# Moving one pair of maxima, one transpose and four scores in the instruction order of an attention kernel

## The chip, the cores and the metric

The kernel runs on one core of a Trainium2 chip. The metric is the device time of one execution in microseconds (us): the median of three executions, 1805.07 us, between 1804.39 and 1807.82.

## What is computed

Four layers in turn on a sequence of 2048 rows of width 640, with 32 heads of 20 columns each. Layers A are linear attention. Layers B split the sequence into four segments of 512 rows; each segment has causal softmax attention within itself, and reads a memory that the earlier segments filled. The part of the reference that the change touches is the attention inside a segment:

```
for s in range(N):
    qs, ks, vs = q[:, :, s], k[:, :, s], v[:, :, s]
    logits = jnp.einsum("bhqd,bhkd->bhqk", qs, ks) * scale + mask
    p = _softmax(logits, axis=-1)
    a_dot = jnp.einsum("bhqk,bhkd->bhqd", p, vs)
    ...
    o = g * a_mem + (1.0 - g) * a_dot
```

## The kernel before

**Two streams on one core.** `attend` runs the softmax attention; `dense` runs everything else (projections, memories, the A layers, output products). `run` interleaves the two. After each stretch of attention, which yields the constant SLOT = 2420, it lets the dense stream go on until its own counted cost has caught up. So PE's order is written by hand: the `manual_schedule` of `build` fixes PE's order to that of the code, while a scheduler orders the instructions of the other engines and of SP's queue.

**Groups.** In each of the two B layers, each of the four segments has eight groups of four heads, so 64 groups in all. A group goes through these operations:

- `stacks` (L985) loads the queries and keys, `qs` and `ks`, with four DMAs in SP's queue. There are three buffers of each.
- `row_max` ("max", L999 on PE, L1006 on DVE) computes plain scores into PSUM banks on PE; DVE reads them and keeps each row's maximum in `mg`. Entries 0 and 2 have two matmuls of 512 columns, entries 1 and 3 have two of 384 and two of 128, entry 4 has four of 256. Each entry takes two banks.
- `split_max` ("split", L1015 and L1016 on DVE) writes the maxima in two f16 parts into a small tile.
- `max_rows` ("rows", L1024 on PE, L1026 on ACT, L1029 in SP's queue) turns these parts with a transpose on PE (`pm`, one bank); ACT copies them to `mt`, and two small DMAs put them into spare rows of `qs`. From then on a score matmul subtracts the maximum itself.
- `scores` ("exp", L1041 on PE, L1045 on ACT, L1052 on POOL) computes transposed scores into a bank, ACT takes the exponential into a tile `pe`, POOL masks the diagonal. Entries 0 and 1 have two banks each, with one matmul of 512 columns in each bank; entries 2 and 3 have two banks each, with matmuls of 384 and 128 columns; entry 4 has two banks, each with two matmuls of 256.
- `weigh` ("sum", L1068) multiplies the values by the exponentials, four heads side by side, into one bank `pv`: part 0 has 512 columns, part 1 384, part 3 128, part 2 256. Only part 2 reads the tiles of "exp" 4.
- `evacuate` ("copy", L1074 on ACT) and `normalize` ("out", L1081 on PE, L1084 and L1091 or L1088 on DVE) bring the result back.

**The order.** An iteration of `attention` works on three groups at once, the newest (0), the one before (1) and the one before that (2), in three stretches, given by a table:

```python
STRETCHES = [[("exp", 4, 2), ("max", 0, 0), ("max", 1, 0), ("rows", 0, 1), ("sum", 0, 2), ("sum", 1, 2), ("sum", 3, 2),
              ("sum", 2, 2), ("copy", 0, 2)],
             [("out", 0, 2), ("max", 2, 0), ("max", 3, 0), ("exp", 0, 1), ("exp", 1, 1)],
             [("exp", 2, 1), ("exp", 3, 1), ("max", 4, 0), ("split", 0, 0), ("load", 0, 0)]]
```

The first number is the entry, the second the group. The maxima that a group's third stretch splits are turned by "rows" in the first stretch of the next iteration; "exp" 0 in its second stretch is the first that needs them.

**Banks.** PSUM has eight banks for all of this and for the dense stream as well:

```python
    def bank(self):
        return self.ps.tile([P, 512], F32, tag="ps", name="ps", bufs=8)
```

A matmul that opens a bank waits until ACT or DVE has read what lay there last. Dense work on PE around these places are the projections (L374, L388), transposes (L313, L876) and memory products (L443, L557, L884).

Of the kernel before, what the change touches and what calls it, by code (L numbers as in the profile page):

```python
# [51 lines left out]
EXPS += [[((0, a, 2, 0), (1, a, 2, 256)) for a in range(2)]]  # L52


STRETCHES = [[("exp", 4, 2), ("max", 0, 0), ("max", 1, 0), ("rows", 0, 1), ("sum", 0, 2), ("sum", 1, 2), ("sum", 3, 2),
              ("sum", 2, 2), ("copy", 0, 2)],
             [("out", 0, 2), ("max", 2, 0), ("max", 3, 0), ("exp", 0, 1), ("exp", 1, 1)],
             [("exp", 2, 1), ("exp", 3, 1), ("max", 4, 0), ("split", 0, 0), ("load", 0, 0)]]


# [70 lines left out]
class Kernel:  # L131
# [965 lines left out]
    def attention(self, segs):  # L1097
# [3 lines left out]
        while n < NSEG * NG or prev or old:  # L1101
# [7 lines left out]
            n += 1  # L1109
            for stretch in STRETCHES:  # L1110
                for op, k, back in stretch:
# [216 lines left out]
```

## Time and profile before

| | |
|---|---|
| median of three executions | 1805.07 us |
| the profiled execution, its own time | 1807.6 us |
| its span, from the first to the last instruction | 1805.9 us |
| PE busy in it | 1699.7 us, 94% |
| DVE, ACT, POOL busy | 66%, 54%, 29% |
| mean granted clock of TensorE | 0.993 |
| attention's matmuls | from 348.9 us to 1779.0 us |

"PE" is matmuls, "PEld" weight loads, "DVE" VectorE, "ACT" ScalarE, "POOL" GpSimd, and "SPq" the DMA queue of SyncE. A row of the waits reads: who waited, at which tile and line, for whom; then the sum of those waits in us, how often, and the longest. A row of the groups reads: line, engine, operation, tiles written <- read, shape, count; then us busy and mean ns of one; then the idle time of the engine just before them, and what ended it. A row of the timeline reads: start in us, length in us, engine, line and operation, and in brackets the idle time before it.

### The profile page before, as it was taken

What the parts mean: (1) busy time and instruction counts of PE and PEld (TensorE: products, weight loads), DVE (VectorE), ACT (ScalarE), POOL (GpSimd) and SP (SyncE); (2) the same over time, 40 slices, a digit from 0 to 9 for tenths busy, and PEclk for the clock granted to TensorE, in tenths of its full rate; (3) what the DMA queues carried; (4) which work ended last, traced back from release to release, by engine and by line L of the source; (5) the groups of instructions that cost most, each with busy time, mean ns of one, the idle gap of its engine ahead of it and who ended that gap; (6) DMA issues with size and microseconds to landing.
All of it is one profiled execution on the core that took longest, in us unless ns stands there. A gap on an engine that the chain in (4) does not pass through costs nothing.

```text
span 1805.9 us, 36393 instructions
## 1 busy us (share of the span) xinstructions
PE 1699.7 (94%) x13032; PEld 1053.8 (58%) x13032; DVE 1185.8 (66%) x3856; ACT 967.7 (54%) x1818; POOL 521.2 (29%) x982
## 2 busy tenths in 40 slices
PE   6999999999999999999989999999989999999998
PEld 4666666654565566455546777666446545644555
DVE  8554444577777677658764466737777777777773
ACT  4454433356546645567656553333665565565664
POOL 1533450012123312333342211221421432233442
PEclk9999999999999999999999999999999999999999
DMA  7332353412322322342211303433122222223432
GB/s 251 142 135 97 139 182 112 141 64 76 108 68 66 108 93 74 114 160 95 79 41 38 110 30 118 174 112 124 56 93 78 97 87 95 96 78 101 132 105 88
DMA packets 118333, 187.61 MB, mean 104 GB/s; under 512 B 13948, under 2 KB 79612, under 8 KB 115848
## 3 DMA queue, kind: packets, MB, share of 16 engines
q1 hardware_dynamic: 105896, 142.68, 24.5%
q0 software_dynamic: 3040, 21.63, 3.3%
q10 hardware_dynamic: 9216, 20.98, 3.0%
q8 instruction: 103, 1.69, 0.4%
q14 instruction: 78, 0.64, 0.1%
HBM read 106.05 MB, written 78.64 MB: 102 GB/s over the span
## 4 chain that ended last, share of the span: by engine, by line
PE 74%; DVE 12%; ACT 6%; issue 3%; POOL 2%; DMA 2%; SPq 0%; ACTq 0%; DVEq 0%; POOLq 0%
PE ps L388 32%; PE ps L374 15%; PE ps L1068 7%; DVE junk L1006 5%; PE ps L313 3%; PE ps L1041 3%; PE ps L557 3%; ACT pe L1045 3%; PE ps L443 2%; PE ps L999 2%; PE ps L884 1%; PE ps L1081 1%; PE ps L723 1%; POOL e L414 1%; DVE nat L849 1%
## 5 line engine op out<-in xcount | busy, mean ns | idle before, releaser
L1006 DVE CUSTOM_DVE_ANT_0 junk<-ps,maskw 128x512 bf16<-128x512 f32 (+3 forms) x1024 | 498.7, 487 | 83.1 <-PE ps L999 26.5
L1045 ACT ACTIVATE pe<-ps,lsc 128x512 f32<-128x512 f32 x640 | 394.1, 693 | 114.6 <-PE ps L1041 112.1
L1052 POOL TENSOR_SCALAR_AFFINE_SELECT pe<-pe 128x256 f32<-128x256 f32 (+1 forms) x640 | 233.7, 371 | 433.6 <-ACT pe L1045 428.0
L388 PEld LDWEIGHTS <-xT 128*128 128x128 f16 x2880 | 282.1, 99 | 121.0 <-issue 9.2
L388 PEld LDWEIGHTS <-oT 128*128 128x128 f16 x1920 | 185.8, 98 | 82.8 <-issue 7.9
L1068 PE MATMUL ps<-pe,v 128*32 128x512 f32 (+3 forms) x2048 | 158.1, 439 | 13.1 <-ACT pe L1045 6.8
L1041 PE MATMUL ps<-qs,ks 62*128 62x384 f16 (+3 forms) x1024 | 133.2, 300 | 24.3 <-DVE mg L1006 11.9
L388 PE MATMUL ps<-w_Bo,oT 128*128 128x320 f16 x960 | 142.3, 301 | 3.2 <-ACT oT L317 1.2
L374 PE MATMUL ps<-xT,w_Bq 128*128 128x512 f16 x600 | 141.5, 382 | 0.7 <-DVE oT L318 0.4
L388 PE MATMUL ps<-w_Bv,xT 128*128 128x320 f16 x960 | 140.9, 301 | 0.1
L388 PE MATMUL ps<-w_Ak,xT 128*128 128x320 f16 x960 | 138.4, 302 | 0.5 <-ACT r L402 0.5
L374 PE MATMUL ps<-xT,w_Bk 128*128 128x512 f16 x600 | 138.8, 379 | 0.0
L999 PE MATMUL ps<-ks,qs 60*128 60x512 f16 (+3 forms) x1024 | 112.5, 297 | 8.6 <-ACT pe L1045 4.1
L1068 PEld LDWEIGHTS ps<-pe,v 128*32 128x32 f32 x2048 | 66.0, 110 | 82.6 <-issue 62.6
L849 DVE SCALAR_TENSOR_TENSOR nat<-ps,nat 128x512 f16<-128x512 f32 x80 | 55.2, 690 | 86.2 <-ACT nat L848 82.2
L414 POOL TENSOR_SCALAR e<-e 128x320 f32<-128x320 f32 (+1 forms) x52 | 82.1, 1579 | 88.7 <-ACT e L410 84.7
L848 ACT ACTIVATE nat<-ps 128x512 f16<-128x512 f32 x80 | 48.0, 600 | 93.3 <-PE ps L374 73.0
L374 PEld LDWEIGHTS <-w_Bq 128*128 128x128 f16 x600 | 56.8, 98 | 69.7 <-issue 9.7
L374 PEld LDWEIGHTS <-w_Bk 128*128 128x128 f16 x600 | 57.0, 98 | 66.4 <-issue 5.9
L1074 ACT ACTIVATE oTf<-ps,cg 128x512 f32<-128x512 f32 x64 | 43.9, 687 | 92.1 <-PE ps L1068 92.0
L421 ACT ACTIVATE v<-ps 128x320 f32<-128x320 f32 x96 | 41.8, 437 | 94.9 <-PE ps L388 91.2
L336 POOL TENSOR_TENSOR rs<-rs,mhalf 128x1 f32<-128x1 f32 x48 | 26.4, 552 | 226.3 <-DVE rs L335 213.5
(220 smaller groups left out, 2677.8 us busy)
## 6 DMA issues: line engine op xcount, KB each, us to landing
x<-xn ACTq DMA_DIRECT2D x48, 320.0 KB
qs<-qd SPq DMA_DIRECT2D x128, 120.0 KB
ks<-kd SPq DMA_DIRECT2D x128, 120.0 KB
xo<-x SPq DMA_DIRECT2D x48, 320.0 KB
pqi<-pqd SPq DMA_DIRECT2D x32, 320.0 KB
qd<-nat SPq DMA_DIRECT2D x40, 256.0 KB
kd<-nat SPq DMA_DIRECT2D x40, 256.0 KB
x<-in_A_x SPq DMA_DIRECT2D x16, 320.0 KB
```

The lines of the kernel that those rows point to most:

```text
L313: nc.tensor.transpose(pt[:, (c - c0) * P:(c - c0 + 1) * P], src[:, c * P:(c + 1) * P], self.ident)
L374: nc.tensor.matmul(p, w[:, c, a, t * P:(t + 1) * P], xT[:, c, b, :], start=k == 0, stop=k == 3 * C - 1)
L388: nc.tensor.matmul(p, xT[:, c, a, i * P:(i + 1) * P], w[:, c, b, n * HN:(n + 1) * HN], start=k == 0, stop=k == 3 * C - 1)
L414: nc.gpsimd.tensor_scalar(e, e, 1.0, eps, op0=OP.min, op1=OP.add)
L557: nc.tensor.matmul(p, xs[:, i, a, c * P:(c + 1) * P], pk[i][:, b, cols], start=k == 0, stop=k == 3 * NT - 1)
L849: nc.vector.scalar_tensor_tensor(nat[:, 1], p, QK_SHIFT, nat[:, 0], op0=OP.mult, op1=OP.subtract)
L999: nc.tensor.matmul(bs[par][:, a:a + n], qs[r, p, i * P:(i + 1) * P], ks[r, p, :n], start=True, stop=True)
L1006: nc.vector.tensor_tensor_reduce(junk[:, :n], bs[par][:, a:a + n], self.maskw[:, SEG - n:], 1.0, NEG, OP.add, OP.max, G["mg"][:, par, p, i ...
L1041: nc.tensor.matmul(b[:, a:a + n], ks[r, p, j * P:(j + 1) * P], qs[r, p, j * P:], start=True, stop=True)
L1045: nc.scalar.activation(e, b, AF.Exp, scale=self.lsc)
L1052: nc.gpsimd.affine_select(d, d, pattern=pat, compare_op=OP.is_ge, fill=0.0, base=0, channel_multiplier=-1)
L1068: nc.tensor.matmul(G["pv"][32 * h4:32 * h4 + 32, j * P:], v[j][:, h * E1:h * E1 + 32], G.pop((p, par, j)), start=j == 0, stop=j == 2, skip ...
```

## The change

Three entries of the table change their places; no operation is added or dropped. In the first stretch, "rows" goes behind "sum" 0, and "max" 2 comes in from the second stretch, as the last entry. In the second stretch the scores "exp" 0 and 1 stand ahead of "max" 3.

```diff
-STRETCHES = [[("exp", 4, 2), ("max", 0, 0), ("max", 1, 0), ("rows", 0, 1), ("sum", 0, 2), ("sum", 1, 2), ("sum", 3, 2),
-              ("sum", 2, 2), ("copy", 0, 2)],
-             [("out", 0, 2), ("max", 2, 0), ("max", 3, 0), ("exp", 0, 1), ("exp", 1, 1)],
+STRETCHES = [[("exp", 4, 2), ("max", 0, 0), ("max", 1, 0), ("sum", 0, 2), ("rows", 0, 1), ("sum", 1, 2), ("sum", 3, 2),
+              ("sum", 2, 2), ("copy", 0, 2), ("max", 2, 0)],
+             [("out", 0, 2), ("exp", 0, 1), ("exp", 1, 1), ("max", 3, 0)],
              [("exp", 2, 1), ("exp", 3, 1), ("max", 4, 0), ("split", 0, 0), ("load", 0, 0)]]
```

On PE, at the end of a first stretch (`m` is the tile with the split maxima, `v` a tile of values, + is new and - is old):

```order
 L999 MATMUL ps<-ks_2760,qs 128x128
+L1068 MATMUL ps<-pe,v_79 32x512 x4
 L1024 LDWEIGHTS m_4094
 L1024 MATMUL pm<-ident_70,m_4094 32x128
-L1068 MATMUL ps<-pe,v_79 32x512 x4
 L1068 MATMUL ps<-pe,v_80 32x384 x4
 L1068 MATMUL ps<-pe,v_82 32x128 x4
 L1068 MATMUL ps<-pe,v_81 32x256 x4
+L999 LDWEIGHTS qs
+L999 MATMUL ps<-ks_2760,qs 128x512
```

The transpose L1024 has moved behind the four matmuls of the first weighing, and the two plain scores of 512 columns (the second one follows in the same form) stand behind the last weighing.

On PE, in the second stretch that follows:

```order
 L1081 MATMUL ps<-ident,oTf 128x128 x4
-L999 LDWEIGHTS qs
-L999 MATMUL ps<-ks_2760,qs 128x512
...
+L1041 LDWEIGHTS ks_2759
+L1041 MATMUL ps<-qs,ks_2759 128x512
...
 L999 LDWEIGHTS qs
 L999 MATMUL ps<-ks_2760,qs 128x384
```

The four scores L1041 follow the transposes of `normalize` directly; the plain scores of 384 and 128 columns, which stood ahead of them, now end the stretch.

In SP's queue, where the scheduler sets the order, around the two DMAs of the turned maxima (L1029):

```order
 L985 DMA ks_2760<-kd 60x2x512
-L985 DMA qs<-qd 60x2x512
-L1029 DMA qs<-mt 2x8x128 x2
-L985 DMA qs<-qd 60x2x512
-L985 DMA ks_2760<-kd 60x2x512
+L985 DMA qs<-qd 60x2x512 x2
+L985 DMA ks_2760<-kd 60x2x512
+L1029 DMA qs<-mt 2x8x128 x2
```

All four loads of a later group now stand ahead of the two small DMAs, where two of the four stood ahead before. Counted over the whole queue, that is so in 42 of the 64 groups now and in 7 before.

## The prediction

> **What bounds the kernel now.** I read the page first: PE is busy nearly all the time, so only the time in which it stands idle can be won, since no work is added or taken away.
>
> ```profile
> span 1805.9 us, 36393 instructions
> PE 1699.7 (94%) x13032; PEld 1053.8 (58%) x13032; DVE 1185.8 (66%) x3856; ACT 967.7 (54%) x1818; POOL 521.2 (29%) x982
> ```
>
> That leaves 1805.9 - 1699.7 = 106.2 us. Next the waits of PE alone, for whom it waits there:
>
> ```profile
> PE ps L1041 <- DVE mg L1006: 11.9, 26, 0.8
> PE ps L313 <- DMA x<-in_A_x: 10.9, 1, 10.9
> PE pm L1024 <- DVE m L1016: 8.3, 12, 0.9
> ...
> PE ps L1068 <- ACT pe L1045: 6.8, 18, 0.7
> PE ps L1068 <- POOL pe L1052: 4.4, 7, 1.2
> ...
> PE ps L1041 <- DMA qs<-mt: 2.0, 1, 2.0
> ```
>
> The largest wait in the attention is that of scores (L1041) for DVE's reading of maxima (L1006). A score does not use a new group's maxima: it waits for the bank. The second row is the start of the kernel, which the change does not touch. Then the groups with shapes kept apart, where the number behind the second bar is PE's idle time just before them:
>
> ```profile
> L1068 PE MATMUL ps<-pe,v 128*32 128x512 f32 x512 | 68.5, 603 | 9.0 <-ACT pe L1045 6.8 <-ACT xn L465 0.6 <-DVE mg L1006 0.5
> L1041 PE MATMUL ps<-qs,ks 62*128 62x512 f16 x256 | 66.8, 377 | 23.0 <-DVE mg L1006 11.6 <-DMA qs<-mt 2.0 <-DVE otok L1088 1.9
> L1041 PE MATMUL ps<-qs,ks 62*128 62x384 f16 x256 | 37.3, 330 | 1.0 <-ACT pe L1045 1.0
> L1024 PE MATMUL pm<-ident,m 128*32 128x128 f16 x64 | 14.5, 226 | 12.2 <-DVE m L1016 8.3 <-ACT r L412 1.2 <-ACT v L421 0.8
> ```
>
> The 512-column scores are those of the second stretch (entries 0 and 1): 23.0 us. Those of 384 columns, in the third stretch, have 1.0. So the second stretch itself makes the wait. The transpose of the maxima has 12.2 us, and the first weighing just behind it 9.0. These 44.2 us are what the change works on. One iteration shows how they arise, PE first, from the end of a first stretch (L1041 with 256 columns) to the scores of the second:
>
> ```profile
> 1590.00 0.40 PE L1041 MATMUL ps<-qs,ks 62*128 62x256 f16 x4
> 1590.23 0.60 PE L999 MATMUL ps<-ks,qs 60*128 60x512 f16 x6
> 1590.77 0.23 PE L1024 MATMUL pm<-ident,m 128*32 128x128 f16 x1
> 1591.32 2.36 PE L1068 MATMUL ps<-pe,v 128*32 128x512 f32 x32 [0.33 <-ACT pe L1045]
> 1593.62 1.47 PE L374 MATMUL ps<-xT,w_Bq 128*128 128x512 f16 x6
> 1594.92 0.60 PE L1081 MATMUL ps<-ident,oTf 128*128 128x128 f32 x4
> 1595.45 0.61 PE L999 MATMUL ps<-ks,qs 60*128 60x512 f16 x6
> 1595.90 0.38 PE L1041 MATMUL ps<-qs,ks 62*128 62x512 f16 x2
> 1597.10 0.79 PE L1041 MATMUL ps<-qs,ks 62*128 62x512 f16 x2 [0.82 <-DVE mg L1006]
> ```
>
> and DVE in the same time (its last reading of the first stretch, then what follows):
>
> ```profile
> 1590.65 0.69 DVE L1006 CUSTOM_DVE_ANT_0 junk<-ps,maskw 128x512 bf16<-128x512 f32 x1
> 1591.49 0.69 DVE L1006 CUSTOM_DVE_ANT_0 junk<-ps,maskw 128x512 bf16<-128x512 f32 x1
> ...
> 1594.20 0.08 DVE L1006 DVE_READ_ACCUMULATOR2_ANT mg<- 128x1 f32 x1
> 1595.56 0.26 DVE L1084 RECIPROCAL rc<-ps 128x16 f32<-128x16 f32 x1 [1.28 <-PE ps L1081]
> 1595.75 0.69 DVE L849 SCALAR_TENSOR_TENSOR nat<-ps,nat 128x512 f16<-128x512 f32 x1
> 1596.36 0.68 DVE L1006 CUSTOM_DVE_ANT_0 junk<-ps,maskw 128x512 bf16<-128x512 f32 x1
> 1596.96 0.08 DVE L1006 DVE_READ_ACCUMULATOR2_ANT mg<- 128x1 f32 x1
> ```
>
> The old second stretch opens 1 + 2 + 2 + 4 = 9 banks (out, maxima 2 and 3, scores), one more than there are. The third score therefore takes a bank whose maxima are read in the same stretch: DVE ends that at 1597.04, PE starts at 1597.10. Just before, DVE had stood idle for 1.28 us.
>
> **Term 1, the second stretch.** With maxima 2 gone ahead, the stretch opens 1 + 4 + 2 = 7 banks, and the scores come before the two of maxima 3. Maxima 2 fall into DVE's hole: its readings end at 1594.28, and two of 512 columns, which follow each other at 1591.49 - 1590.65 = 0.84 us, take 1.7 us, so they would end at 1596.0. The third score is due at 1595.90 + 0.38 = 1596.28, less 0.61 - 0.38 = 0.23 for the maxima 3 that no longer stand ahead: just in time, even if it took one of their banks. From 23.0 us go the 2.0 for a DMA, which the change does not cure, and the 1.0 that the 384-column scores still have: 20.0 is the most; 0 is the least, if the wait only moves (second rival). I take 17, near the upper end, less 3 for iterations where dense work fills DVE's hole. Two rows of ACT in the first stretch, the exponentials of exp 4 and the copy to `mt`:
>
> ```profile
> 1590.49 1.27 ACT L1045 ACTIVATE pe<-ps,lsc 128x512 f32<-128x512 f32 x2 [0.39 <-PE ps L1041]
> 1591.65 0.25 ACT L1026 ACTIVATE mt<-pm 32x128 f16<-32x128 f16 x1
> ```
>
> The two banks more that this stretch now takes are free by the time: ACT has read those of exp 4 at 1590.49 + 1.27 = 1591.76, the last weighing ends at 1593.68; I cost them at nothing. Maxima 3 start later by the scores' length, 0.38 + 0.79 us, and the split needs them one stretch on. That too costs nothing as long as dense work (here L374) lies between; if not, it comes back at L1024, less the 1.07 us that now cover it (below).
>
> **Term 2, rows behind the first weighing.** The 512-column weighing covers 68.5 / 64 = 1.07 us per group, more than the longest wait of 0.9 for the parts (`m`); so the 8.3 us vanish, as does the wait for the second bank: what the pair now needs first is only one bank, that of the old transpose, whose waits of 12.2 - 8.3 = 3.9 us stay. 12.2 + 9.0 - 3.9 = 17.3 is the most. But in this stretch a chain runs beside PE: exp 4, ACT, POOL, last weighing.
>
> ```profile
> PEld ps L1068 <- POOL pe L1052: 18.9, 49, 1.7
> ```
>
> In 49 iterations the weights of a weighing already wait for POOL, 0.39 us each on average. PE that comes sooner may only wait there: the least is 0. I take 10, nearer the upper end because PE itself idles for POOL only 4.4 us in 7.
>
> **Term 3, the maxima's way to the scores.** Transpose, ACT, two DMAs, then the scores. In the iteration above, SP's queue:
>
> ```profile
> 1590.42 0.32 SPq L985 DMA_DIRECT2D ks<-kd  x1
> 1590.91 0.32 SPq L985 DMA_DIRECT2D qs<-qd  x1
> 1591.92 1.28 SPq L1029 DMA_DIRECT2D qs<-mt  x2
> 1593.26 0.41 SPq L985 DMA_DIRECT2D qs<-qd  x1
> 1593.71 0.46 SPq L985 DMA_DIRECT2D ks<-kd  x1
> ```
>
> The transpose comes 1.07 us later. But ACT was busy with the exponentials until 1591.76 anyway, so `mt` starts not at 1591.65 but at about 1590.77 + 1.07 + 0.23 = 1592.07: 0.4 later. ACT waits 0.3 us for it; queued behind is the copy of `pv` (L1074), which needs the last weighing's end anyway. The scores come 0.2 sooner. So of 1595.90 - 1591.92 = 3.98 us from issue to scores, 3.4 stay. What the DMAs need is bounded by the shortest distance that I found without a wait, issue 954.05 to scores 957.53, 3.48 us:
>
> ```profile
> 954.05 1.27 SPq L1029 DMA_DIRECT2D qs<-mt  x2
> ```
> ```profile
> 957.53 0.60 PE L1041 MATMUL ps<-qs,ks 62*128 62x512 f16 x4
> ```
>
> So the margin is between 0.1 below zero and some tenths above. Also, two more loads of SP's queue now stand ahead: 0.41 + 0.46 us of issue, which fit in the time that SP waits for `mt` (from 1591.23 to 1591.92, and 0.4 more). What they carry goes ahead of the rows. At their size, and the best rate on the page,
>
> ```profile
> GB/s 251 142 135 97 139 182 112 141 64 76 108 68 66 108 93 74 114 160 95 79 41 38 110 30 118 174 112 124 56 93 78 97 87 95 96 78 101 132 105 88
> ...
> qs<-qd SPq DMA_DIRECT2D x128, 120.0 KB
> ```
>
> that is up to 2 x 120 / 251 = 1.0 us, at least 0 where they were away before. The Trainium skill, "DMA: Bandwidth & Descriptors", section "Queues, rings and completion order", speaks against this change: on each DMA engine descriptors are consumed in ring order. By that rule the rows would wait out the loads, and the whole 1.0 us would count in every group: 1805 - 27 + 70 = 1848. No row here shows such a delay by itself. I take 3 us in all (a few groups short by some tenths); ends 0 and 64 x (3.48 - 3.4 + 1.0) = 70 us.
>
> **The sum.** 17 + 10 - 3 = 24 us. I hand a quarter back: dense steps behind each removed stall wait for ACT and DVE with margins that the stall had widened. 18 us remain. The profiled execution's span falls from 1805.9 to 1788 (its own time 1807.6 to 1790); on the median, 1805.07 - 18 = 1787.
>
> **Rivals.** *The rows arrive too late (slower).* If the scores wait 0.5 us more in every group, half of the 1.0 above, that is 32 us against 18 won: 1805 + 14 = 1819. For it: the window shrinks in every group, and the loads moved ahead. Against it: one wait of 2.0 us in 64 groups today, and ACT takes up half the delay. It decides where issue to landing takes over about 3.3 us.
>
> *DVE's work only moves (little faster).* No reading gets shorter; if DVE reaches maxima 2 late, or maxima 3 hold up the split, half of term 1 and most of term 2 come back: 1805 - 7 = 1798. For it: DVE 66% busy over the span, with dense work put between maxima by the scheduler. Against it: the hole of 1.28 us. The Trainium skill, "TensorEngine Tiling (Array Packing)", section "PSUM Bottleneck", says that packing speeds up TensorE but not the reading of PSUM; by that rule this case would win.
>
> *Nothing is left.* The scheduler orders ACT, DVE and SP anew throughout, and new small waits eat what was won: 1805.
>
> **How the numbers follow.** Forecast (1776 to 1795) 0.58; DVE's work moves (1795 to 1801) 0.17; nothing left 0.12; rows too late 0.13. About 0.2%, 3.6 us, is what a measurement can tell from no change here. So faster 0.75, same 0.12, slower 0.13. For 8 in 10 I leave out what lies under 1774 (nearly all of both upper ends, 37 us, won) and most of the late rows: 1774 to 1806.
>
> **What would show it.** Right: idle before the 512-column scores falls from 23.0 to about 5, before L1024 and the 512-column weighing from 21.2 to about 10, with PE's busy time unchanged near 1700. Wrong: a row of scores waiting for the DMA of `mt` over 10 us (first rival); scores still waiting for DVE, or L1024 for the split (second); the weighing waiting for POOL well over 4.4 us (term 2).

## The result, and the profile after

The changed kernel takes 1765.53 us (median of six executions, 1763.05 to 1769.35), the kernel before 1806.03 us beside it. The ratio is 0.9768, with a 95% interval of 0.9754 to 0.9782: 40 us faster, where 18 were forecast and 1774 was the range's lower end. The direction was right, the size was not. One of the six executions of the kernel before took 2189.03 us; without it their median is 1805.12 us. The profiled execution of the changed kernel took 1769.35 us.

The head of the page after, the span first, then busy time, share and instructions of each engine:

```profile
span 1767.6 us, 36360 instructions
PE 1683.3 (95%) x13032; PEld 1050.2 (59%) x13032; DVE 1195.1 (68%) x3856; ACT 971.2 (55%) x1818; POOL 517.4 (29%) x982
```

The span fell by 1805.9 - 1767.6 = 38.3 us. PE's idle time fell from 106.2 to 1767.6 - 1683.3 = 84.3, which is 21.9 of them. The other 16.4 us came out of PE's *busy* time, with the same 13032 matmuls. The prediction had said that nothing could be won there. PE's largest waits after:

```profile
PE ps L313 <- ACT xh L361: 19.7, 5, 11.3
PE pm L1024 <- DVE m L1016: 5.0, 2, 3.2
PE ps L1041 <- DMA qs<-mt: 3.7, 2, 2.9
PE ps L999 <- DVE mg L1006: 3.6, 10, 0.5
PE ps L1068 <- POOL pe L1052: 3.4, 7, 1.4
...
PE ps L999 <- ACT pe L1045: 3.1, 10, 0.6
```

The wait of scores for DVE's reading of maxima, 11.9 us before, has left the list. The first row lies ahead of the attention, in the kernel's first 121 us; before, the same line waited 10.9 us for a DMA and 7.7 for ACT. The groups by shape (the number behind the first bar is busy time, the one behind the second the idle time just before):

```profile
L1068 PE MATMUL ps<-pe,v 128*32 128x512 f32 x512 | 68.2, 603 | 4.6 <-ACT r L412 1.7 <-ACT pe L1045 0.9 <-ACT r L402 0.7
L999 PE MATMUL ps<-ks,qs 60*128 60x384 f16 x256 | 51.6, 324 | 6.1 <-DVE mg L1006 2.3 <-ACT pe L1045 1.6 <-DVE tmp L1091 0.8
L1041 PE MATMUL ps<-qs,ks 62*128 62x512 f16 x256 | 40.4, 385 | 3.8 <-DMA qs<-mt 3.7
L999 PE MATMUL ps<-ks,qs 60*128 60x128 f16 x256 | 33.5, 216 | 0.0
L1024 PE MATMUL pm<-ident,m 128*32 128x128 f16 x64 | 14.1, 221 | 5.2 <-DVE m L1016 5.0 <-DVE oT L318 0.2
```

The 512-column scores lost 23.0 - 3.8 = 19.2 us of idle time, and 66.8 - 40.4 = 26.4 us of busy time, while one of them still takes 385 ns (377 before). So they are not shorter; they overlap more. One iteration after, on PE, shows how:

```profile
1545.14 0.60 PE L999 MATMUL ps<-ks,qs 60*128 60x512 f16 x6
1545.67 1.06 PE L1068 MATMUL ps<-pe,v 128*32 128x512 f32 x8
1546.55 0.22 PE L1024 MATMUL pm<-ident,m 128*32 128x128 f16 x1
1546.56 1.51 PE L1068 MATMUL ps<-pe,v 128*32 128x384 f32 x24
1548.00 0.39 PE L999 MATMUL ps<-ks,qs 60*128 60x512 f16 x2
1548.32 2.21 PE L388 MATMUL ps<-w_Bv,xT 128*128 128x320 f16 x15
1550.37 0.60 PE L1081 MATMUL ps<-ident,oTf 128*128 128x128 f32 x4
1550.90 0.61 PE L1041 MATMUL ps<-qs,ks 62*128 62x512 f16 x4
1551.34 0.38 PE L999 MATMUL ps<-ks,qs 60*128 60x384 f16 x4
```

All four scores stand in one row of 0.61 us, and the next matmul starts 1551.34 - 1550.90 = 0.44 us after the first. Before, they stood in two rows of 0.38 and 0.79 us with 0.82 between. A score uses 62 rows of PE, and the scores of a pair use different halves (rows from 0 and from 64), so two run at a time. Counted over the records of all 64 groups, the fourth score started 0.99 us after the first before, and 0.25 after: 0.74 x 64 = 47 us, of which the trace books less than half as idle.

The rest is a wait too. Each score opens a bank of its own, so the fourth waits for another bank than the third. In the iteration of the prediction the third started at 1597.10, and the fourth 0.79 - 0.38 = 0.41 us later, at 1597.51. In between, at 1596.96 + 0.49 = 1597.45, DVE ended its reading of the bank of `normalize`:

```profile
1596.96 0.49 DVE L1091 TENSOR_TENSOR tmp<-ps,rc 128x320 f32<-128x320 f32 x1
```

By the records of the kernel before, the fourth score lagged the third in 60 of the 64 groups, and in 59 of these it started 0.04 to 0.05 us after an instruction of DVE or ACT that it waits for had ended; in nearly half of the groups the third had not waited at all. In all, the fourth lagged the third by 28.3 us before and by 1.2 after. Of the 28.3 us only 6.5 were idle time; for the other 21.8 the third score ran, and PE counted as busy. In the same way the third started 18.7 us later behind the second than it does now, of which 13.5 were idle and 5.2 lay under the first pair. So 21.8 - 1.2 + 5.2 = 25.8 of the 26.4 us of busy time that went were waits under a score that still ran.

The transpose L1024 shows the same on a smaller scale: it now lies inside the weighings' rows; before, it ran out alone and PE then stood.

### The profile page after: what moved, and what is told of

Read it like the earlier page. It is cut to its first block, busy times and chain, and to the rows that moved or that the text cites. A ratio compares the mean times of both kernels' runs of the same rounds, so it can differ in the third digit from the quotient of the medians.

```text
span 1767.6 us, 36360 instructions
## 1 busy us (share of the span) xinstructions
PE 1683.3 (95%) x13032; PEld 1050.2 (59%) x13032; DVE 1195.1 (68%) x3856; ACT 971.2 (55%) x1818; POOL 517.4 (29%) x982
## 3 DMA queue, kind: packets, MB, share of 16 engines
q1 hardware_dynamic: 105896, 142.68, 25.5%
## 4 chain that ended last, share of the span: by engine, by line
PE 73%; DVE 12%; ACT 6%; issue 3%; DMA 3%; POOL 2%; SPq 0%; ACTq 0%; DVEq 0%; POOLq 0%
PE ps L388 31%; PE ps L374 15%; PE ps L1068 6%; DVE junk L1006 4%; PE ps L1041 3%; PE ps L313 3%; PE ps L999 3%; ACT pe L1045 3%; PE ps L557 3%; PE ps L443 3%; PE ps L884 1%; PE ps L1081 1%; PE ps L723 1%; DMA qs<-mt 1%; DVE st L331 1%
## 5 line engine op out<-in xcount | busy, mean ns | idle before, releaser
L1052 POOL TENSOR_SCALAR_AFFINE_SELECT pe<-pe 128x256 f32<-128x256 f32 (+1 forms) x640 | 229.6, 365 | 453.6 <-ACT pe L1045 449.3
L999 PE MATMUL ps<-ks,qs 60*128 60x384 f16 (+3 forms) x1024 | 128.8, 298 | 12.5 <-DVE mg L1006 3.6
L1041 PE MATMUL ps<-qs,ks 62*128 62x512 f16 (+3 forms) x1024 | 107.4, 301 | 5.4 <-DMA qs<-mt 3.7
L999 PEld LDWEIGHTS <-qs 60*128 60x128 f16 x1024 | 51.1, 94 | 82.5 <-issue 55.1
```

The costliest lines, as they stand in the source:

```text
L999: nc.tensor.matmul(bs[par][:, a:a + n], qs[r, p, i * P:(i + 1) * P], ks[r, p, :n], start=True, stop=True)
L1041: nc.tensor.matmul(b[:, a:a + n], ks[r, p, j * P:(j + 1) * P], qs[r, p, j * P:], start=True, stop=True)
L1052: nc.gpsimd.affine_select(d, d, pattern=pat, compare_op=OP.is_ge, fill=0.0, base=0, channel_multiplier=-1)
```

## The experiments

**Theory A**: a matmul that has to wait also loses its overlap with its neighbours, and that loss is counted as busy; the missing half of the gain is the pairs of scores. **Rival B**: only idle time counts, and what the forecast missed came from somewhere else, from the rows' new place above all. Times are set against the kernel before on the same chip (1806.61, 1806.47 and 1806.71 us in the three sets). The profiles of all experiments but the one with scores between transposes have line numbers one lower (L1040 is L1041 here, L998 is L999, L1023 is L1024).

### The rows alone

```diff
-... ("max", 1, 0), ("rows", 0, 1), ("sum", 0, 2), ("sum", 1, 2), ...
+... ("max", 1, 0), ("sum", 0, 2), ("rows", 0, 1), ("sum", 1, 2), ...
```

> Only the transpose of the maxima moves behind the first weighing; the second stretch stays as it was. Theory A (a score that waits for a bank also falls out of its pair, and what it loses then is counted as PE busy): only term 2 comes, 7 to 11 us faster than before, near 1797; the 512-column scores keep about 67 us busy and about 23 us idle. Rival B (only PE's idle time counts, and what the forecast missed came from elsewhere, the rows' move with its new order on ACT and SP's queue above all): about 25 us faster, near 1781.

Measured: 1788.33 us, ratio 0.9895 (0.9878 to 0.9911), 18.3 us faster. Neither theory had it: A said 7 to 11, B 25. The page's head and two groups:

```profile
span 1790.2 us, 36392 instructions
PE 1693.4 (95%) x13032; PEld 1048.7 (59%) x13032; DVE 1185.6 (66%) x3856; ACT 971.6 (54%) x1818; POOL 519.8 (29%) x982
```
```profile
L1040 PE MATMUL ps<-qs,ks 62*128 62x512 f16 x256 | 66.8, 377 | 24.5 <-DVE mg L1005 11.3 <-DMA qs<-mt 3.5 <-DVE otok L1087 1.9
L1023 PE MATMUL pm<-ident,m 128*32 128x128 f16 x64 | 14.0, 219 | 0.3 <-DVE oT L317 0.3
```

The scores stayed as they were, 66.8 us busy, as A had it. Idle time fell by 106.2 - (1790.2 - 1693.4) = 9.4 us, near term 2 as forecast; the other 6.3 us of the 15.7 by which the span fell in the profiled execution (the longest of the four) are busy time once more. Counted over the records, the transposes ran with nothing beside them for 7.7 us in the kernel before (0.12 us in each group, between the maxima that had run out and the weighing that waited) and for 0.3 us here. Read so, A holds in a wider form than it was put: not only in pairs, but at any matmul that still runs when a wait begins. That is read from the records alone; no run parts these 6.3 us from the rest of what moved.

### Maxima 2 alone

```diff
-             [("out", 0, 2), ("max", 2, 0), ("max", 3, 0), ("exp", 0, 1), ("exp", 1, 1)],
+             [("out", 0, 2), ("max", 3, 0), ("exp", 0, 1), ("exp", 1, 1)],
```

with `("max", 2, 0)` put at the end of the first stretch.

> Only maxima 2 move to the end of the first stretch; maxima 3 still stand ahead of the scores, and the rows stay in the old place. The second stretch then opens 7 banks before it has to wait for one of its own. Theory A: about 25 us faster than before, near 1781; busy time of the 512-column scores falls from 66.8 to 40 to 45 us and their idle time to about 6. Rival B: the idle time falls in the same way, busy time hardly, and the gain is 12 us or less, near 1794.

Measured: 1780.40 us, ratio 0.9855 (0.9839 to 0.9872), 26.2 us faster. The groups:

```profile
L1040 PE MATMUL ps<-qs,ks 62*128 62x512 f16 x256 | 42.7, 376 | 3.7 <-DMA qs<-mt 1.8 <-DVE mg L1005 0.9 <-DVE tmp L1090 0.4
L1023 PE MATMUL pm<-ident,m 128*32 128x128 f16 x64 | 14.6, 228 | 16.9 <-DVE m L1015 13.2 <-ACT r L411 1.4 <-ACT pkt L877 0.6
```

Idle time of the scores fell by 19.3 us and busy time by 24.1, as A said. B allowed 12 us in all; it falls here. The transposes' idle time rose from 12.2 to 16.9 us, that for the split from 8.3 to 13.2.

### The scores ahead of the maxima, alone

```diff
-             [("out", 0, 2), ("max", 2, 0), ("max", 3, 0), ("exp", 0, 1), ("exp", 1, 1)],
+             [("out", 0, 2), ("exp", 0, 1), ("exp", 1, 1), ("max", 2, 0), ("max", 3, 0)],
```

> Only the order within the second stretch changes: scores, then maxima 2, then maxima 3. The bank that is short is then short for the maxima (L999). Theory A: the pairs of the scores are whole, their busy time falls to about 40 us; the last maxima wait instead, part of it as idle time at L999 and part as broken pairs of the matmuls of 384 and 128 columns, so 15 to 25 us faster, near 1785. Rival B: the wait only moves, idle time at L999 rises by 10 us or more, and the gain is under 8 us, near 1800.

Measured: 1807.30 us, ratio 0.9999 (0.9989 to 1.0008): no change. B's number came true, and idle time moved to L999 as it said; but busy time, which B leaves where it was, moved with it:

```profile
L998 PE MATMUL ps<-ks,qs 60*128 60x384 f16 x256 | 62.2, 324 | 14.4 <-ACT pe L1044 9.5 <-DVE mg L1005 1.7 <-DVE oT L317 0.6
L998 PE MATMUL ps<-ks,qs 60*128 60x128 f16 x256 | 39.5, 218 | 0.0
L1040 PE MATMUL ps<-qs,ks 62*128 62x512 f16 x256 | 39.4, 383 | 2.4 <-DMA qs<-mt 2.4
```

In the kernel before, maxima 3 had these rows:

```profile
L999 PE MATMUL ps<-ks,qs 60*128 60x384 f16 x256 | 45.6, 321 | 2.0 <-ACT pe L1045 0.9 <-DVE oT L318 0.6
...
L999 PE MATMUL ps<-ks,qs 60*128 60x128 f16 x256 | 30.1, 216 | 0.0
```

The scores won 27.4 us of busy and 20.6 of idle time. Maxima 3, now last, lost 62.2 - 45.6 + 39.5 - 30.1 = 26.0 of busy and 14.4 - 2.0 = 12.4 of idle time, and maxima 4 and the transposes a few more. Here too the busy part is in the main a wait under a running matmul: by the records the second matmul of 384 columns lags the first by 18.3 us in all, by 0.2 in the kernel before, and in 54 of 64 groups it starts as an instruction of ACT or DVE that it waits for has just ended. The whole loss, with its busy part, went to the next pair that lacked a bank. A's forecast of the time was wrong: I had taken broken pairs of maxima to be cheaper.

### The change without the rows

The changed table, with `("rows", 0, 1)` back in front of `("sum", 0, 2)`.

> The whole change but for the rows, which stay behind maxima 1. Theory A: all of term 1 with the pairs, about 30 us faster than before, near 1775, some 8 to 11 us above the changed kernel; 512-column scores near 40 us busy, 4 idle, and L1024 with the 512-column weighing near 21 us idle as before. Rival B: 15 us faster or less, near 1790.

Measured: 1777.00 us, ratio 0.9832 (0.9817 to 0.9847), 29.6 us faster, as A said. The scores stand at 39.6 us busy and 2.0 idle. The transposes and the weighing behind them wait 17.8 + 8.2 = 26.0 us, more than the 21.2 of before, which A had expected:

```profile
L1067 PE MATMUL ps<-pe,v 128*32 128x512 f32 x512 | 70.8, 622 | 8.2 <-ACT pe L1044 5.5 <-DVE mg L1005 0.9 <-ACT xn L464 0.6
L1023 PE MATMUL pm<-ident,m 128*32 128x128 f16 x64 | 14.6, 228 | 17.8 <-DVE m L1015 15.0 <-ACT r L411 1.4 <-ACT r L401 0.5
```

The prediction feared that maxima 3, later by the scores' length, would hold up the split. Little of the rise is theirs: with maxima 2 alone moved, and maxima 3 in their old place, the same two rows already stand at 16.9 + 8.6 = 25.5 us. What makes the rest of it was not tried by itself. The rows' new place covers most of these waits in the full change (5.2 + 4.6).

### Seven banks

```diff
-        return self.ps.tile([P, 512], F32, tag="ps", name="ps", bufs=8)
+        return self.ps.tile([P, 512], F32, tag="ps", name="ps", bufs=7)
...
-        pt = self.ps.tile([P, 1024], F16, tag="ps", name="pm", bufs=8)
+        pt = self.ps.tile([P, 1024], F16, tag="ps", name="pm", bufs=7)
```

> The changed kernel with seven PSUM banks instead of eight, so that the second stretch is one bank short again, as it was before the change. Theory A: the lost time shows in two ways, as idle time before matmuls that open a bank and as broken pairs, with PE's busy time in the rows of scores and maxima (L1041, L999) at least 15 us up; the kernel comes near the old one, 1795 or more. Rival B: busy time stays within 5 us, all of the loss is idle time.

Measured: 1810.73 us, ratio 1.0025 (1.0015 to 1.0035): one bank is worth more than the whole change. As A said: busy time of the eight groups of scores and maxima together rose from 298.4 to 317.3 us, by 18.9, and PE's idle time by 27 us. The pairs that broke are those of maxima 3, which stand last in the stretch:

```profile
L998 PE MATMUL ps<-ks,qs 60*128 60x384 f16 x256 | 60.4, 325 | 16.6 <-ACT pe L1044 9.3 <-DVE tmp L1090 1.9 <-DVE otok L1087 0.9
L1040 PE MATMUL ps<-qs,ks 62*128 62x512 f16 x256 | 41.1, 382 | 4.8 <-DMA qs<-mt 3.4 <-DVE mg L1005 0.9 <-DVE tmp L1090 0.4
```

### Pairs broken without a wait: scores between transposes

In `normalize`, each of the four transposes is followed by one score; "exp" 0 and 1 are then left out of the second stretch.

```diff
             nc.tensor.transpose(pt[:, i * P:(i + 1) * P], oT[:, i * P:(i + 1) * P], self.ident)
+            if between:
+                self.scores(between, EXPS[i // 2][i % 2])
```

> The changed kernel, with one of the four transposes of the normalization (which use all of PE's rows) written ahead of each of the four 512-column scores, so that no two scores can stand side by side. The work, the banks and the order in which they are opened are the same. In the changed kernel four scores advance PE by 0.49 us (from 1591.82 to 1592.31), or 0.23 us a pair; one after the other they would need four times about 0.22. Theory A (a broken pair costs PE's own time, whatever breaks it): 64 groups by 0.4 to 0.45 us, 26 to 29 us slower than the changed kernel, near 1792, and PE busy up by about as much with idle time unchanged. Rival B (busy time in these rows is only how the records are drawn): within 5 us of the changed kernel, near 1766 to 1771.

Measured: 1812.71 us, ratio 1.0036 (1.0023 to 1.0048), 47 us slower than the changed kernel. PE busy and one group on PE:

```profile
span 1810.6 us, 36332 instructions
PE 1740.0 (96%) x13032; PEld 1062.0 (59%) x13032; DVE 1193.6 (66%) x3856; ACT 973.0 (54%) x1818; POOL 518.3 (29%) x982
```
```profile
1600.79 0.39 PE L1041 MATMUL ps<-qs,ks 62*128 62x512 f16 x1
1601.11 0.33 PE L1081 MATMUL ps<-ident,oTf 128*128 128x128 f32 x1
1601.37 0.39 PE L1041 MATMUL ps<-qs,ks 62*128 62x512 f16 x1
```

Between these rows nothing waits (the group's first score, ahead of them, had waited 0.26 us for its DMA). In the whole kernel PE is busy for 56.7 us longer, its idle time is even 13.7 us lower (70.6), and the kernel is 47 us slower. That busy time is real, and B falls. It is not the loss of the kernel before, though, where the fourth score waited for a bank: here the order itself keeps the scores apart. A's size of 26 to 29 us was too small: a score and the next transpose advance PE by 1601.37 - 1600.79 = 0.58 us. In the changed kernel a transpose advances it by (1550.90 - 1550.37) / 4 = 0.13, and a score of a pair by 0.11. Two scores that only ran one after the other would take about 0.22 each (0.44 us for two pairs), so 0.58 - 0.13 - 0.22, some 0.2 us, come on top for each change to all rows and back; the split of these 0.58 us is an estimate from the two traces.

### Another order of the halves

```diff
-EXPS = [[((p, a, 0, 0),) for a in range(2)] for p in range(2)]
+EXPS = [[((p, a, 0, 0),) for p in range(2)] for a in range(2)]
```

> The changed kernel, with the four scores of 512 columns written in another order: the two of one half of PE's rows first, then the two of the other half. Nothing waits for a bank that did not wait before; only the neighbours are of the same half, so that no more than the middle two can run at once. Theory A (the time of a broken pair is PE's own time and counts in full): four of them take about 0.83 us instead of 0.61, their busy time rises from 40 to about 54 us, PE's idle time stays, and the kernel is about 13 us slower than the changed one, near 1779. Rival B (busy time in these rows is only how the records are drawn, only idle time counts): within 4 us of the changed kernel, near 1766.

Measured: 1764.93 us, ratio 0.9770 (0.9756 to 0.9785), the changed kernel's time. This does not speak for B, since the edit did not break the pairs:

```profile
1591.72 0.61 PE L1040 MATMUL ps<-qs,ks 62*128 62x512 f16 x4
1592.20 0.32 PE L998 MATMUL ps<-ks,qs 60*128 60x384 f16 x1
```

Four scores still take 0.61 us and advance PE by 0.48. So the second half must have run beside the first, though it was written behind it. As a test of A against B the run is void; it shows that neighbours need not alternate.

### The rows behind the copy

```diff
-... ("sum", 0, 2), ("rows", 0, 1), ("sum", 1, 2), ("sum", 3, 2), ("sum", 2, 2), ("copy", 0, 2), ...
+... ("sum", 0, 2), ("sum", 1, 2), ("sum", 3, 2), ("sum", 2, 2), ("copy", 0, 2), ("rows", 0, 1), ...
```

> The changed kernel with the transpose of the maxima still later, behind the copy: 24 matmuls, about 1.5 us, more on PE before it. The distance from the issue of the two small DMAs to the scores, 4.0 us in the median of the changed kernel's 64 groups, falls to about 2.5. If they need 3.48 us, as the prediction had it, 42 groups run short, 54 us in all: near 1819. If they need about 2.1, the shortest distance without a long wait in the changed kernel, 18 groups run short, 7 us in all, and the 5.0 us before the transpose go: within 10 us of the changed kernel, 1762 to 1775.

Measured: 1777.87 us, ratio 0.9847 (0.9833 to 0.9862), 12 us above the changed kernel and 41 below what 3.48 us would have made. SP's queue and PE in one group, and the scores' row:

```profile
1564.88 0.42 SPq L984 DMA_DIRECT2D ks<-kd  x1
1567.28 1.28 SPq L1028 DMA_DIRECT2D qs<-mt  x2
```
```profile
1569.09 0.39 PE L1040 MATMUL ps<-qs,ks 62*128 62x512 f16 x1 [0.61 <-DMA qs<-mt]
1569.75 0.60 PE L1040 MATMUL ps<-qs,ks 62*128 62x512 f16 x3 [0.28 <-DMA qs<-mt]
```
```profile
L1040 PE MATMUL ps<-qs,ks 62*128 62x512 f16 x256 | 51.6, 386 | 11.8 <-DMA qs<-mt 11.5
```

The first score starts 1569.09 - 1567.28 = 1.81 us after the first issue; of the 29 scores that wait, 27 start 1.80 to 1.86 us after the issue of one of the two DMAs, and two 4.9 and 3.0. The second DMA goes out some 0.66 us later and fills the other half, whose score starts 0.66 us later. So the need is 1.81 us from each issue outside those two groups, not 3.48. My second theory had 2.1 and at most 1775 us, and missed by 3 us; what it lacked is that the two DMAs land apart and break the pair: 51.6 - 40.4 = 11.2 us busy beside 8.0 idle.

### Maxima 3 at other places

The second stretch of the changed kernel, with maxima 3 first; in the middle; or at the head of the third stretch:

```diff
-             [("out", 0, 2), ("exp", 0, 1), ("exp", 1, 1), ("max", 3, 0)],
+             [("out", 0, 2), ("max", 3, 0), ("exp", 0, 1), ("exp", 1, 1)],
```

> The changed kernel, but maxima 3 stay ahead of the scores, so that only the rows and maxima 2 move. Theory: the two parts alone gave 18 and 26 us; the order of the scores and maxima 3 is what keeps the changed kernel from the sum, since maxima 3 at the end of the stretch find their banks late (their pairs broken, 9 us more busy) and hold up the split: so about 44 us faster than before, near 1762, with L999 of 384 columns back at 46 us busy. Rival: the parts overlap anyway, because both free the same wait; then 1766 as the changed kernel, or some us more for the 2 to 3 us of broken pairs in the scores.

Measured: 1766.74 us, ratio 0.9784 (0.9769 to 0.9799). The rival held: 39.7 us, not the 18.3 + 26.2 = 44.5 of the parts. L998 of 384 columns came back to 46.1 us, and the scores paid for it:

```profile
L1040 PE MATMUL ps<-qs,ks 62*128 62x512 f16 x256 | 46.4, 376 | 7.5 <-DMA qs<-mt 3.3 <-DVE mg L1005 2.5 <-DVE tmp L1090 0.7
L998 PE MATMUL ps<-ks,qs 60*128 60x384 f16 x256 | 46.1, 327 | 3.6 <-DVE mg L1005 2.1 <-DVE oT L317 0.6 <-ACT pe L1044 0.5
```

So the third part of the change, scores ahead of maxima 3, shows no gain once the other two are made.

```diff
-             [("out", 0, 2), ("exp", 0, 1), ("exp", 1, 1), ("max", 3, 0)],
+             [("out", 0, 2), ("exp", 0, 1), ("max", 3, 0), ("exp", 1, 1)],
```

> The changed kernel with maxima 3 between the first and the second pair of scores. Theory: each bank-opening step then has a pair ahead of it, and the broken pairs are spread: neither L999 of 384 columns (51.6 us busy now) nor the second pair of scores (40.4 for both) is fully paid: 1760 to 1766. Rival: whichever comes last in the stretch waits, so the sum is the same as with maxima 3 last or first: 1765 to 1768.

Measured: 1763.33 us, ratio 0.9758 (0.9745 to 0.9770). It is the lowest of all, but its interval overlaps the changed kernel's, so no gain is shown.

```diff
-             [("exp", 2, 1), ("exp", 3, 1), ("max", 4, 0), ("split", 0, 0), ("load", 0, 0)]]
+             [("max", 3, 0), ("exp", 2, 1), ("exp", 3, 1), ("max", 4, 0), ("split", 0, 0), ("load", 0, 0)]]
```

(and maxima 3 taken out of the second stretch)

> The changed kernel with maxima 3 at the head of the third stretch. In the changed kernel their matmuls of 384 and 128 columns have 9 us more busy and 4 us more idle time than before; behind a slice of dense work their banks are free. Theory: these 13 us are won, less what maxima 3 and 4 now hold up the split by (L1024 waited 5.0 us for it): 1757 to 1765. Rival: the third stretch then opens eight banks without a pause, and the loss comes back there, at the scores of 384 columns and maxima 4: 1768 or more.

Measured: 1811.86 us, ratio 1.0022 (1.0013 to 1.0032). My theory was wrong by 47 us or more, and the rival right: eight banks opened in one stretch leave the last of them, maxima 4, waiting for exponentials, and push the split back.

```profile
L998 PE MATMUL ps<-ks,qs 60*128 60x256 f16 x256 | 36.6, 272 | 25.1 <-ACT pe L1044 13.1 <-DVE oT L317 3.2 <-ACT r L411 2.1
L1023 PE MATMUL pm<-ident,m 128*32 128x128 f16 x64 | 14.3, 223 | 10.8 <-DVE m L1015 10.8
```

## Why the prediction was wrong

**The step that failed** is the first one: that only the time in which PE stands idle can be won, and that PE's busy time would stay near 1700. It fell to 1683.3. The idle time fell by 21.9 us where the sum said 18; what the sum lacked is the 16.4 us of busy time in the profile. In its place the runs showed that a wait can lie under a matmul that still runs: the prediction named the wait of the third score for its bank and missed that the fourth waits for one of its own, 27.1 us over the 64 groups, of which 20.6 were booked as busy. The working had the evidence in hand: two rows of two scores, 0.38 and 0.79 us long, against one row of four in 0.60 us at 957.53, quoted for another purpose. The Trainium skill, "Perfetto Trace Analysis", section "Identifying the Most-Contended Engine", says that matmul busy time is not a good measure of how close a kernel is to its roofline, and points to the busy time of weight loads as one of two better ones. The trace agrees on the first: the matmuls' busy time fell by 16.4 us with the work unchanged, while that of the weight loads stayed at 1053.8 and 1050.2 us, 58% and 59%. The reason that the Trainium skill gives there, that pipelined matmuls look smaller in the trace, is another one than the hidden wait here.

**Term 1** was right in mechanism and in its idle part (17 forecast, 19.2 measured with the DMA's wait in it), and mis-sized as a whole: 26.4 us of busy time, nearly all of it waits under a running score, come on top. Of these 9.4 go back at the pairs of maxima 3 (L999 of 384 and 128 columns, 6.0 + 3.4 us busy), with 4.1 us of idle time.

**Term 2**: idle time fell from 21.2 to 5.2 + 4.6 = 9.8, so 11.4 where 10 was taken. The rows alone are worth 18.3 us as a time. In their profiled execution the span fell by 15.7, of which 9.4 were idle time; the rest is put down above to the transpose, which no longer runs out alone.

**Term 3** was small, as taken (3 us), but for another reason. The wait for the DMA rose from 2.0 to 3.7 us, in two groups. The need is 1.81 us from issue, not 3.48: the shortest distance that I had found without a wait was only the shortest that occurred. The rule of ring order that the prediction cites from the Trainium skill ("DMA: Bandwidth & Descriptors", "Queues, rings and completion order") would have cost 1.0 us in each group. The trace of the changed kernel does not show that price in a group like this one, the loads and the rows on SP's queue, then the scores on PE:

```profile
1422.07 0.32 SPq L985 DMA_DIRECT2D ks<-kd  x1
1422.50 0.81 SPq L985 DMA_DIRECT2D qs<-qd  x2
1423.36 0.42 SPq L985 DMA_DIRECT2D ks<-kd  x1
1423.95 1.28 SPq L1029 DMA_DIRECT2D qs<-mt  x2
```
```profile
1426.90 0.60 PE L1041 MATMUL ps<-qs,ks 62*128 62x512 f16 x4
```

All four loads go out within 1.9 us ahead of the rows, and 2.95 us later the scores start without waiting. Whether the rows were held up by up to 2.95 - 1.81 = 1.14 us behind the loads can't be told from that; if they were, the window hid it. With the rows behind the copy the window is short enough to tell: in the group shown there the last load was issued 1567.28 - 1564.88 = 2.40 us ahead of the rows, in the group at 936.67 us none in the 5 us ahead, and both scores started 1.81 us after the issue. So loads issued 2.4 us ahead or earlier cost the rows nothing there; for loads 0.6 us ahead, as in the group above, it stays open. The two groups that wait, at 721 and 853 us, took 6.6 and 4.4 us from issue to scores, and the same two took 4.9 and 3.0 with the rows behind the copy. There the rule may bite; no run took the loads away from them.

**The quarter handed back** (6 us) was about right in idle time: 19.2 + 11.4 = 30.6 won in the two places, 21.9 in all, so 8.7 came back (L999 of 384 columns 4.1, dense matmuls the rest).

**The rivals.** Late rows needed issue to landing over 3.3 us and got 1.81, outside the two groups above. "DVE's work only moves" came true in part, at maxima 3 and in the 5.0 us before the transpose. The overlap of the parts (18.3 for the rows and 29.6 for the rest make 47.9, against 40.5 for both) lies there for the most part: the transpose waits 0.3 us with the rows alone and 5.2 in the full change.

The busy time adds up roughly: 26.4 us won at the scores and about 7 at the transposes, 9.4 given back at maxima 3, and about 6.5 at maxima 2, whose pair now lies between weighings and dense matmuls and by the records runs with nothing beside it for that much longer; 17.5 against 16.4. The sum is rough, since two of its terms (scores, maxima 3) are the time that rows cover and two (transposes, maxima 2) the time in which nothing runs beside them. The last of these terms is read from the records alone and was not tried by itself.

## What to carry to other kernels

Price a wait by what PE advances, from the start of one matmul to the start of the next, not by the idle time in front of it; a wait that lies under a matmul still running is booked as work, as that of the fourth score here. Where equal groups of matmuls stand in rows of different counts and lengths (x2 and x2 here, x4 there), compare those rows first. Then count the banks that a stretch opens before any is free again: one pair too many cost 23 to 30 us here in the second stretch (1788.33 - 1765.53 with the rows moved, 1807.30 - 1777.00 without) and 46 in the third (1811.86 - 1765.53). Moving a pair across other work gave it back; reordering within the second stretch alone did not.

## What the runs showed of the hardware

**Halves of PE run on their own.** With both scores of one half written first, four still took 0.61 us. The Trainium skill, "TensorEngine Tiling (Array Packing)", section "Key Properties", says that tiles execute independently; the trace agrees.

**Changing between full and half matmuls costs.** Transposes and scores in turn advanced PE by 1.94 us in a group (median, from the first transpose to the matmul behind the last score), against 0.98 us in blocks of four: 0.97 us more, where the lost pairs alone explain about 0.43 (an estimate: two pairs at 0.22 us). The same section of the Trainium skill says that a change of tiling mode drains TensorE; the rest, about 0.5 us for six more changes, is in keeping with that, though no run shows the drain apart from the order.

**A small DMA was there in 1.81 us**, from its issue in SP's queue to the start of the matmul that waits for it (1.80 to 1.86 in 27 of the 29 waits with the rows behind the copy, 4.9 and 3.0 in the other two), and the second of two issued together followed by the 0.66 us of its issue.
